# RWKV attention, a bilinear layer and a SoLU layer in one kernel: the second layer's transposes go to the DMA crossbar

## Chip, cores and metric

The kernel runs on one core of one Trainium2 chip. The metric is the device time of one launch in microseconds (us). The kernel before takes 664.51 us, the median of 3 runs (663.81 to 665.28).

## The reference, cut to what matters

```python
def _attn_ref(r, k, v, w, u):              # B, H, S, D = 4, 8, 768, 48
    for t in range(S):
        ...
        y[:, :, t] = np.einsum('bhd,bhde->bhe', rt, state + cur)
        state = w[None, :, :, None] * state + np.einsum('bhd,bhe->bhde', kt, vt)

def _moe_ref(x, w1, w2, w3, w_out):        # x: 3072 x 384, d_ff = 1024
    return ((x @ w1) * (x @ w2) @ w3) @ w_out

def _moe2_ref(x, w_in, w_out, g_ln):       # the "second layer", w_in 384 x 1024, w_out 1024 x 384
    h = x @ w_in
    e = np.exp(h - np.max(h, axis=-1, keepdims=True))
    sm = e / (np.sum(e, axis=-1, keepdims=True) + 1e-09)
    solu = h * sm
    mu = np.mean(solu, axis=-1, keepdims=True)
    var = np.mean((solu - mu) ** 2, axis=-1, keepdims=True)
    return ((solu - mu) / np.sqrt(var + 1e-06) * g_ln) @ w_out
```

Everything is float32. The change lies in `_moe2_ref` alone: between `solu - mu` (the "centred products") and the product with `w_out`.

## The kernel before, in words

The 3072 tokens are 24 chunks of 128 (NCH = 24). The first part of the kernel (attention and the bilinear layer) follows an order that a planner writes out; it ends near 440 us and is not touched. Its result, x for the second layer, lies in SBUF with features on the partitions. Every product is made of 32-bit floats split into a high and a low part (`split`, L525: ScalarE copies the high part into the fp32r type, VectorE subtracts it from the source for the low part), and `mm3` (L195) adds three matmuls per term: high by high, high by low, low by high (L199, L200, L201).

The second layer is the loop of L1170 over i, under a manual schedule: each engine runs its instructions in the order in which the code issues them, and waits only on semaphores. The steps are:

- `split_chunk(i + 2)`: x of the chunk two ahead is split, high part by ScalarE (`x2h`, L841), low part by GpSimd (`x2l`, L842).
- `s3(i + 1)`: 18 matmuls of 512 columns (2 halves, 3 k-tiles, 3 products) write `ps_h`, 128 tokens x 1024. VectorE takes the negated maximum (`nm`, L856), ScalarE the exponential `e` and its sum (L859), VectorE the product `p` (L863), its mean and variance (L866 to L876), GpSimd the factor `al` (L878, L880).
- `s4(i - 1)`: 24 matmuls of 384 columns (8 k-tiles, 3 products) of the transposed chunk with w_out, into `ps_o`; ScalarE scales the result by `al` into `o` (L920), and SyncE's queue (SP) stores it (L921).
- `turn(i)`, which is `s4_T(i)`: TensorE transposes the centred chunk with the identity, 8 blocks of 128x128 into two banks `ps_p` (L900); ScalarE and VectorE split each half out of PSUM into `pt` (L902).
- `center(i + 1)`: ScalarE writes p minus the mean over `e` (L885).

On TensorE the order of an iteration is thus s3(i + 1), s4(i - 1), T(i). The first iteration has T(0) between the halves of s3(1), the last one issues T(22) right behind the exponential of chunk 23, ahead of that chunk's statistics (`at == 2`, L860). After the loop come three quarters of s4(22), T(23), the last quarter, and s4(23).

Pools alternate by chunk parity (`pick(i)`): two `ps_h`, two `e`, two `p`; `pt` alternates between two places.

Of the kernel before, what the change touches and what calls it, by code (L numbers as in the profile page):

```python
# [8 lines left out]
F32 = mybir.dt.float32  # L9
F32R = mybir.dt.float32r  # L10
I32 = mybir.dt.int32
U32 = mybir.dt.uint32
AF = mybir.ActivationFunctionType
ALU = mybir.AluOpType
AX = mybir.AxisListType
# [108 lines left out]
def tile_rwkv_bilinear_solu(  # L124
# [19 lines left out]
    nc = tc.nc  # L144
    B, S, H, D = r.shape
    P = 128
    DP = 64
    NC = S // P
    NCH = B * NC
# [4 lines left out]
    KF = FF // P  # L154
    GT = B * P
    NH = FF // 2

    const = ctx.enter_context(tc.tile_pool(name="const", bufs=1, side="left"))
# [33 lines left out]
    def f32(ap):  # L192
        return ap.bitcast(F32)

    def mm3(dst, terms, start=True, stop=True):  # L195

        last = len(terms) - 1
        for i, ((ah, al), (bh, bl)) in enumerate(terms):
            nc.tensor.matmul(dst, lhsT=ah, rhs=bh, start=start and i == 0, stop=False)  # L199
            nc.tensor.matmul(dst, lhsT=ah, rhs=bl, start=False, stop=False)  # L200
            nc.tensor.matmul(dst, lhsT=al, rhs=bh, start=False, stop=stop and i == last)  # L201
# [37 lines left out]
    def same(n):  # L239

        return max([m for m in range(n) if slot(m) == slot(n)], default=-1)
# [94 lines left out]
    def diag(n, e=nc.vector):  # L336

        asb = asb_of(n)
        if e is nc.scalar:
            for h in range(H):  # L340
                nc.scalar.activation(asb[:, h, :], ident, AF.Copy, scale=bon[n][:, h:h + 1])
        else:
# [5 lines left out]
    def copy(e, dst, src):  # L348
        (e.copy if e is nc.scalar else e.tensor_copy)(dst, src)  # L349
# [134 lines left out]
    def cv_m(i):  # L484
        n = units[i][1][0] * units[i][1][1]
        hi = work[i]["s"][:, 0:n, 1].bitcast(F32)
        if i < NPS:
            m = psx.tile([P, UW], F32, name="cvp", tag=f"ps_x2{i % 3}")
            nc.scalar.activation(m[:, 0:n], hi, AF.Copy, scale=2.0 ** -112)
        else:  # L490
            m = cv.tile([P, UW], F32, name="cvm", tag="cvm", bufs=cmb)
            nc.scalar.activation(m[:, 0:n], hi, AF.Abs, scale=2.0 ** -112)
        work[i].update(m=m, mi=m[:, 0:n].bitcast(I32))

    def cv_q(i):
        n = units[i][1][0] * units[i][1][1]
        q = cv.tile([P, UW], I32, name="cvq", tag="cvq", bufs=cqb)
        nc.scalar.activation(q[:, 0:n], work[i]["s"][:, 0:n, 0].bitcast(U32), AF.Copy, scale=2.0 ** -29)
        work[i]["q"] = q[:, 0:n]
# [25 lines left out]
    def split(src, h, l):  # L525
        return (lambda e=nc.scalar: copy(e, h, src)), (lambda e=nc.vector: e.tensor_sub(l, src, f32(h)))  # L526

    def run(fns):
        for fn in fns:
            fn()  # L530
# [243 lines left out]
    def open_phase2():  # L774
# [14 lines left out]
        def split_wo(f, i):  # L789
            h, l = d2["woh"][:, i:i + 1, :], d2["wol"][:, i:i + 1, :]  # L790
            return (
                lambda: nc.scalar.activation(h, f, AF.Copy, scale=gc[:, i:i + 1]),
                lambda: nc.vector.scalar_tensor_tensor(
# [27 lines left out]
    pq = []  # L821
# [13 lines left out]
    def pick(i):  # L835
        return pq[i % len(pq)]
# [8 lines left out]
    def s3(x, i=0, between=None, at=1):  # L845
        xh, xl = x
        wih, wil = d2["wih"], d2["wil"]
        q = pick(i)["q"]
        ph = pick(i)["h"].tile([P, 2, NH], F32, name="ps_h", tag="ps_h")
        for hf in range(2):  # L850
            if between and hf == at:
                between()
            hsl = slice(hf * NH, (hf + 1) * NH)
            mm3(ph[:, hf, :], [((xh[:, kt, :], xl[:, kt, :]), (wih[:, kt, hsl], wil[:, kt, hsl])) for kt in range(KM)])
        nm = q.tile([P, 1], F32, name="nm", tag="nm")
        nc.vector.tensor_reduce(out=nm, in_=ph, axis=AX.XY, op=ALU.max, negate=True)  # L856
        e = q.tile([P, 2, NH], F32, name="e", tag="e")
        sm = q.tile([P, 1], F32, name="sm", tag="sm")
        nc.scalar.activation(e, ph, AF.Exp, bias=nm, scale=1.0, accum_out=sm)  # L859
        if between and at == 2:  # L860
            between()
        p = q.tile([P, 2, NH], F32, name="p", tag="p")
        nc.vector.tensor_mul(p, ph, e)  # L863
        st = q.tile([P, 2, 6], F32, name="bst", tag="bst")
        for hf in range(2):
            nc.vector.bn_stats(st[:, hf, :], p[:, hf, :])  # L866
        mv = q.tile([P, 2], F32, name="mv", tag="mv")
        nc.vector.bn_aggr(mv, st)
        nmean = q.tile([P, 1], F32, name="nmean", tag="nmean")
        nc.vector.tensor_scalar_mul(nmean, mv[:, 0:1], -1.0)  # L870
        c1 = q.tile([P, 1], F32, name="c1", tag="c1")
        nc.vector.tensor_scalar_add(c1, sm, 1e-9)
        nc.vector.reciprocal(c1, c1)
        vs = q.tile([P, 1], F32, name="vs", tag="vs")
        nc.vector.tensor_scalar(vs, mv[:, 1:2], c1, c1, op0=ALU.mult, op1=ALU.mult)
        nc.vector.tensor_scalar_add(vs, vs, 1e-6)  # L876
        rs = q.tile([P, 1], F32, name="rs", tag="rs")
        nc.gpsimd.tensor_tensor(rs, vs, pq[0]["nhalf"], op=ALU.pow)  # L878
        a = q.tile([P, 1], F32, name="al", tag="al")
        nc.gpsimd.tensor_mul(a, rs, c1)  # L880
        return e, p, nmean, a, i

    def center(st):
        e, p, nmean, a, i = st
        nc.scalar.activation(e, p, AF.Identity, bias=nmean, scale=1.0)  # L885
        return e, a, i

    def s4_T(pc):
        e, a, i = pc
        pv = e.rearrange("t a f -> t (a f)")  # L890
        if i % len(pq):
            t = const.tile([P, 2, KF, P], F32R, name="pt", tag="ox")
        else:
            t = pq[0]["q"].tile([P, 2, KF, P], F32R, name="pt", tag="pt")
        th, tl = t[:, 0], t[:, 1]
        for hf in range(2):
            ps = pick(hf)["p"].tile([P, KF // 2, P], F32, name="ps_p", tag="ps_p")
            for j in range(KF // 2):
                kf = hf * (KF // 2) + j
                nc.tensor.transpose(ps[:, j, :], pv[:, kf * P:(kf + 1) * P], ident)  # L900
            sl = slice(hf * (KF // 2), (hf + 1) * (KF // 2))
            run(split(ps, th[:, sl, :], tl[:, sl, :]))  # L902
        return th, tl, a, i

    def s4_mm(pT, ps, part, parts):
        th, tl = pT[:2]
        woh, wol = d2["woh"], d2["wol"]
        if part == 0:
            ps = pq[-1]["p"].tile([P, DM], F32, name="ps_o", tag="ps_o", bufs=len(pq))
        kfs = range(part * KF // parts, (part + 1) * KF // parts)  # L910
        mm3(
            ps, [((th[:, kf, :], tl[:, kf, :]), (woh[:, kf, :], wol[:, kf, :])) for kf in kfs],
            start=part == 0, stop=part == parts - 1,
        )
        return ps

    def s4_out(pT, ps, dst):
        a, i = pT[2:]
        o = pick(i)["q"].tile([P, DM], F32, name="o", tag="o")
        nc.scalar.activation(o, ps, AF.Copy, scale=a)  # L920
        nc.sync.dma_start(dst, o)  # L921

    def s4(pT, dst):
        s4_out(pT, s4_mm(pT, None, 0, 1), dst)

    def split_chunk(i):
        if i < NCH:
            xs[i] = x2_split(x2s(i).rearrange("t o m e -> t (o m) e"))

    def out_rows(i):  # L930
        c, b = divmod(i, B)
        row = b * S + c * P
        return out[row:row + P, :]

    xs, sm, pT = {}, {}, {}
    qsb, qps = ExitStack(), ExitStack()


# [28 lines left out]
    for n in range(NA + 2):  # L967
# [5 lines left out]
        p = same(n)  # L973
# [141 lines left out]
    for c in range(NG, NC):  # L1115
        last = c == NC - 1
        for ft in range(KF):
# [33 lines left out]
            if last and ft == KF - 1:  # L1151
                st = s3(xs[0])
# [14 lines left out]
    def turn(i):  # L1167
        pT[i] = s4_T(sm[i])

    for i in range(NCH - 1):  # L1170
        split_chunk(i + 2)
        within = i in (0, NCH - 2)
        st = s3(xs[i + 1], i + 1, (lambda: turn(i)) if within else None, 2 if i else 1)
        if i > 0:
            s4(pT[i - 1], out_rows(i - 1))
        if not within:
            turn(i)
        sm[i + 1] = center(st)
    ok = nc.values_load(wok[0:1, 0:1], min_val=0, max_val=1)
    i = NCH - 1  # L1180
    ps = None
    for j in range(4):
        if j == 3:
            turn(i)
        ps = s4_mm(pT[i - 1], ps, j, 4)
    s4_out(pT[i - 1], ps, out_rows(i - 1))
    s4(pT[i], out_rows(i))
    qps.close()
    qsb.close()
    sched.close()  # L1190
# [2 lines left out]
    with tc.If(ok < 1):  # L1193
# [8 lines left out]
        st = rp.tile([P, DE, D], F32, name="state")  # L1202
# [11 lines left out]
        with tc.For_i(0, S, TB) as t0:  # L1214
# [4 lines left out]
            for g in range(E4):  # L1219
                for b in range(B):  # L1220
                    sl = slice(g * BH + b * H, g * BH + (b + 1) * H)
# [24 lines left out]
        with tc.For_i(0, B * S, P) as row:  # L1246
# [6 lines left out]
            ps = pq[0]["p"].tile([P, KM, P], F32, name="ps_p", tag="ps_p")  # L1253
# [6 lines left out]
            for ft in range(KF):  # L1260
# [4 lines left out]
                a = gp.tile([P, P], F32, name="a")  # L1265
# [9 lines left out]
            xf = gp.tile([P, KM, P], F32, name="xf")  # L1275
            nc.scalar.copy(xf, px)
            s4(s4_T(center(s3(x2_split(xf)))), out[bass.ds(row, P), :])
        fx.close()
        rec.close()
# [63 lines left out]
```

## Time and profile before

| | |
|---|---|
| median of 3 runs | 664.51 us (663.81 to 665.28) |
| the profiled execution: span from first to last instruction | 662.6 us |
| TensorE busy | 648.3 us, 98% |
| VectorE, ScalarE, GpSimd busy | 411.6, 296.0, 260.1 us |
| DMA, whole kernel | 64.45 MB, mean 97 GB/s |
| second layer's loop | from about 440 us to 657.7 us |

The page gives no other time of the profiled execution than its span; it lies 1.9 us under the median of the unprofiled runs. A matmul's own duration covers its whole way through the array and overlaps its neighbours', so what a matmul costs is read from the distance of two starts, or from the chain of waits, not from its duration.

### The profile page before, as it was taken

Reading aid. Unit: us, or ns where it says so; the run is one execution under the profiler, and the core shown is the slowest. Engines: PE = TensorE matmul, PEld = TensorE weight load, DVE = VectorE, ACT = ScalarE, POOL = GpSimd, SP = SyncE. Lnnn points to the kernel's source line nnn. Section 1 sums busy time; section 2 is a strip of 40 time slices with the busy share of each in tenths; the row PEclk is TensorE's granted clock in tenths of the full one; section 3 lists DMA queues with packets and bytes.
Section 4 is the critical chain, followed back from the end, with each engine's and each line's share of the span. In section 5 each row is a group of like instructions: output and inputs, shape, how many; then the busy total and the mean of one; then the engine's idle time right before and its main releaser. Section 6 shows DMA issues by size and latency. Waiting matters only on the chain.

```text
span 662.6 us, 12211 instructions
## 1 busy us (share of the span) xinstructions
PE 648.3 (98%) x4820; PEld 555.6 (84%) x4820; DVE 411.6 (62%) x731; ACT 296.0 (45%) x600; POOL 260.1 (39%) x267
## 2 busy tenths in 40 slices
PE   8989999999999999999999999999999999999996
PEld 8767779998878888888888887879999999999996
DVE  8999999656753444344433477247666766667653
ACT  5575877553223222322232575344444534445442
POOL 3887655420345444555572555412222112221110
PEclk9999999999999999999999999999999999999999
DMA  8889696525452222222224132000000000000001
GB/s 285 256 281 294 222 301 200 189 90 152 144 155 69 68 68 69 69 68 69 72 81 124 69 119 72 0 1 12 25 25 26 24 13 25 24 25 25 13 24 41
DMA packets 44322, 64.45 MB, mean 97 GB/s; under 512 B 4833, under 2 KB 31202, under 8 KB 44258
## 3 DMA queue, kind: packets, MB, share of 16 engines
q1 hardware_dynamic: 44258, 63.60, 29.7%
q8 instruction: 40, 0.66, 0.4%
q14 instruction: 24, 0.20, 0.1%
HBM read 54.67 MB, written 8.91 MB: 96 GB/s over the span
## 4 chain that ended last, share of the span: by engine, by line
PE 84%; DVE 8%; ACT 2%; DMA 2%; issue 2%; POOL 2%; SPq 0%; DVEq 0%; POOLq 0%; ACTq 0%
PE ps_h L201 5%; PE ps_h L199 5%; PE ps_h L200 5%; PE ps_o L200 5%; PE ps_o L199 5%; PE ps_o L201 5%; PE ps_x L199 5%; PE ps_x L201 4%; PE ps_x L200 4%; PE ps_aa L199 4%; PE ps_bb L199 4%; PE ps_aa L200 4%; PE ps_aa L201 4%; PE ps_bb L200 4%; PE ps_bb L201 4%; PE ps_p L900 3%
## 5 line engine op out<-in xcount | busy, mean ns | idle before, releaser
L726 DVE TENSOR_TENSOR g<-ps_bb,a 128x512 f32<-128x512 f32 x48 | 33.0, 686 | 92.9 <-PE ps_bb L201 92.0
L511 POOL TENSOR_TENSOR cvm<-cvm,cvq 128x384 int32<-128x384 int32 (+1 forms) x54 | 66.8, 1244 | 41.9 <-DVE cvm L507 33.6
L878 POOL TENSOR_TENSOR rs<-vs,nhalf 128x1 f32<-128x1 f32 x24 | 13.0, 543 | 171.6 <-DVE vs L876 171.6
L737 POOL TENSOR_TENSOR gl<-g,gh 128x512 fp32r<-128x512 f32 x32 | 41.2, 1287 | 62.3 <-ACT gh L732 62.3
L199 PE MATMUL ps_o<-woh,pt 128*128 128x384 f32 x192 | 64.3, 335 | 0.0
L200 PE MATMUL ps_o<-wol,pt 128*128 128x384 f32 x192 | 64.3, 335 | 0.0
L201 PE MATMUL ps_o<-woh,pt 128*128 128x384 f32 x192 | 64.2, 334 | 0.0
L349 ACT COPY a<-ps_aa 128x512 f32<-128x512 f32 x46 | 26.9, 585 | 80.6 <-PE ps_aa L201 80.5
L199 PE MATMUL ps_bb<-x,w2h 128*128 128x512 f32 x144 | 57.2, 397 | 3.0 <-DVE g L726 3.0
L859 ACT ACTIVATE e<-ps_h,nm 128x1024 f32<-128x1024 f32 x24 | 26.8, 1117 | 73.2 <-DVE nm L856 73.2
L199 PE MATMUL ps_h<-wih,x2h 128*128 128x512 f32 x144 | 58.5, 406 | 0.0
L199 PE MATMUL ps_x<-gh,wc 128*128 128x512 f32 x144 | 58.3, 405 | 0.0
L199 PE MATMUL ps_aa<-x,w1h 128*128 128x512 f32 x144 | 57.2, 397 | 0.1
L201 PE MATMUL ps_h<-wih,x2l 128*128 128x512 f32 x144 | 56.6, 393 | 0.0
L200 PE MATMUL ps_aa<-x,w1h 128*128 128x512 f32 x144 | 56.2, 390 | 0.3 <-DVE x L526 0.3
L201 PE MATMUL ps_x<-gh,wc 128*128 128x512 f32 x144 | 56.3, 391 | 0.0
L200 PE MATMUL ps_h<-wil,x2h 128*128 128x512 f32 x144 | 56.2, 390 | 0.0
L201 PE MATMUL ps_bb<-x,w2l 128*128 128x512 f32 x144 | 56.1, 390 | 0.0
L201 PE MATMUL ps_aa<-x,w1l 128*128 128x512 f32 x144 | 56.1, 390 | 0.0
L200 PE MATMUL ps_x<-gl,wc 128*128 128x512 f32 x144 | 56.1, 390 | 0.0
L200 PE MATMUL ps_bb<-x,w2h 128*128 128x512 f32 x144 | 56.1, 390 | 0.0
L856 DVE TENSOR_REDUCE nm<-ps_h 128x1 f32<-128x1024 f32 x24 | 29.4, 1224 | 38.8 <-PE ps_h L201 38.8
(169 smaller groups left out, 1569.1 us busy)
## 6 DMA issues: line engine op xcount, KB each, us to landing
cvs<-in_w_T_dram SPq DMA_DIRECT2D x16, 512.0 KB, 4.3
cvs<-in_w_dram SPq DMA_DIRECT2D x16, 384.0 KB, 5.2
kT<-in_k_T_dram SPq DMA_DIRECT2D x20, 256.0 KB, 2.7
rT<-in_r_T_dram SPq DMA_DIRECT2D x20, 256.0 KB, 3.7
v_in<-in_v_dram SPq DMA_DIRECT2D x24, 192.0 KB, 3.9
k_in<-in_k_dram SPq DMA_DIRECT2D x24, 192.0 KB, 3.6
out_dram<-o SPq DMA_DIRECT2D x24, 192.0 KB, 1.9
gd<-g SPq DMA_DIRECT2D x16, 256.0 KB, 2.7
```

What stands on the lines that cost most here:

```text
L199: nc.tensor.matmul(dst, lhsT=ah, rhs=bh, start=start and i == 0, stop=False)
L200: nc.tensor.matmul(dst, lhsT=ah, rhs=bl, start=False, stop=False)
L201: nc.tensor.matmul(dst, lhsT=al, rhs=bh, start=False, stop=stop and i == last)
L349: (e.copy if e is nc.scalar else e.tensor_copy)(dst, src)
L511: nc.gpsimd.tensor_tensor(mi, mi, q, op=ALU.add)
L726: nc.vector.tensor_mul(gt[c, ft], pb, at[c, ft])
L737: e.tensor_sub(gl, g, f32(gh))
L856: nc.vector.tensor_reduce(out=nm, in_=ph, axis=AX.XY, op=ALU.max, negate=True)
L859: nc.scalar.activation(e, ph, AF.Exp, bias=nm, scale=1.0, accum_out=sm)
L878: nc.gpsimd.tensor_tensor(rs, vs, pq[0]["nhalf"], op=ALU.pow)
L900: nc.tensor.transpose(ps[:, j, :], pv[:, kf * P:(kf + 1) * P], ident)
```

## The change

From chunk 2 to chunk 22 (`M0 <= i < M1`, 21 chunks) `s4_T` is no longer called. In its place `move`, right behind `center`, does the following: ScalarE copies the 16-bit halves of `e` apart into the space of `p` (4 copies of 128x512, read with a step of two halves), SP stores each half of the chunk to HBM (256 KB each), and SP issues a transposing DMA for each, which reads rows of 512 16-bit numbers and writes them with features on the partitions back over `e`. `moved`, issued one iteration later, splits that tile from SBUF into `pt`. The product s4 of a chunk comes one iteration later than before. `e` now has three buffers. Chunks 0, 1 and 23 keep `s4_T`.

```diff
@@ s3
-        e = q.tile([P, 2, NH], F32, name="e", tag="e")
+        e = pq[min(i % 3, 1)]["q"].tile([P, 2, NH], F32, name="e", tag=f"e{i % 3}")
...
-        a = q.tile([P, 1], F32, name="al", tag="al")
+        a = q.tile([P, 1], F32, name="al", tag="al", bufs=2)
@@ center
-        return e, a, i
+        return e, a, i, p
+
+    def move(pc):
+
+        e, a, i, p = pc
+        ev = e.bitcast(U16).rearrange("t a (f k) -> t a f k", k=2)
+        pv = p.bitcast(U16).rearrange("t a (k f) -> t a k f", k=2)
+        d = pld.tile([2, P, 2, NH], U16, name="pd", tag="pd", bufs=2)
+        for hf in range(2):
+            for k in range(2):
+                nc.scalar.copy(pv[:, hf, k, :], ev[:, hf, :, k])
+            nc.sync.dma_start(d[hf], pv[:, hf])
+        x = e.rearrange("p a (k t) -> p (a k) t", t=P)
+        xv = x.bitcast(U16)
+        for hf in range(2):
+            sl = slice(hf * (KF // 2), (hf + 1) * (KF // 2))
+            nc.sync.dma_start_transpose(xv[:, sl, :], d[hf].rearrange("t k f -> (t k) f"))
+        return x, a, i
+
+    def pt_tile(i):
+        if i % len(pq):
+            return const.tile([P, 2, KF, P], F32R, name="pt", tag="ox")
+        return pq[0]["q"].tile([P, 2, KF, P], F32R, name="pt", tag="pt")
+
+    def moved(mv):
+        x, a, i = mv
+        t = pt_tile(i)
+        for hf in range(2):
+            sl = slice(hf * (KF // 2), (hf + 1) * (KF // 2))
+            run(split(x[:, sl, :], t[:, 0, sl, :], t[:, 1, sl, :]))
+        return t[:, 0], t[:, 1], a, i
@@ the loop
+    M0, M1 = 2, NCH - 1
     for i in range(NCH - 1):
         split_chunk(i + 2)
-        within = i in (0, NCH - 2)
-        st = s3(xs[i + 1], i + 1, (lambda: turn(i)) if within else None, 2 if i else 1)
-        if i > 0:
-            s4(pT[i - 1], out_rows(i - 1))
-        if not within:
+        st = s3(xs[i + 1], i + 1, None if i else (lambda: turn(0)))
+        if M0 <= i - 1:
+            pT[i - 1] = moved(pT[i - 1])
+        n = i - 1 if i <= M0 else i - 2
+        if n >= 0 and i != M0 + 1:
+            s4(pT[n], out_rows(n))
+        if 0 < i < M0:
             turn(i)
         sm[i + 1] = center(st)
+        if M0 <= i + 1 < M1:
+            pT[i + 1] = move(sm[i + 1])
     ok = nc.values_load(wok[0:1, 0:1], min_val=0, max_val=1)
-    i = NCH - 1
-    ps = None
-    for j in range(4):
-        if j == 3:
-            turn(i)
-        ps = s4_mm(pT[i - 1], ps, j, 4)
-    s4_out(pT[i - 1], ps, out_rows(i - 1))
-    s4(pT[i], out_rows(i))
+    pT[NCH - 2] = moved(pT[NCH - 2])
+    s4(pT[NCH - 3], out_rows(NCH - 3))
+    turn(NCH - 1)
+    for i in (NCH - 2, NCH - 1):
+        s4(pT[i], out_rows(i))
```

## Rows read from the trace of the kernel before

**Rows 1.** The page: busy time of each engine, share of the span, instructions.

```profile
PE 648.3 (98%) x4820; PEld 555.6 (84%) x4820; DVE 411.6 (62%) x731; ACT 296.0 (45%) x600; POOL 260.1 (39%) x267
```

**Rows 2.** Busy time per engine in one stretch of the loop, granted clock, DMA share, GB/s.

```profile
core 0: us, PE busy (x) PEld busy (x) DVE busy (x) ACT busy (x) POOL busy (x), PEclk, DMA share, GB/s
500.00:520.00 20.00, 20.00 (x111) 18.16 (x110) 13.36 (x32) 10.04 (x18) 3.52 (x6) 1.00 0.09 31
```

**Rows 3.** Chain of waits, 495 to 520 us: start, length in us, engine and line.

```profile
499.49 0.87 PE ps_p L900 x8
...
504.27 0.23 PE ps_h L201
...
508.67 0.87 PE ps_p L900 x8
```

**Rows 4.** Timeline of one chunk: start, us, engine, line, operation, idle before.

```profile
504.55 1.22 DVE L856 TENSOR_REDUCE nm<-ps_h 128x1 f32<-128x1024 f32 x1 [1.76 <-PE ps_h L201]
505.80 1.12 ACT L859 ACTIVATE e<-ps_h,nm 128x1024 f32<-128x1024 f32 x1 [3.23 <-DVE nm L856]
508.76 0.58 ACT L920 ACTIVATE o<-ps_o,al 128x384 f32<-128x384 f32 x1 [1.75 <-issue]
509.24 1.06 ACT L349 CAST pt<-ps_p 128x512 fp32r<-128x512 f32 x2
510.18 1.17 ACT L885 ACTIVATE e<-p,nmean 128x1024 f32<-128x1024 f32 x1
510.70 1.28 DVE L526 TENSOR_TENSOR pt<-ps_p,pt 128x512 fp32r<-128x512 f32 x2
511.24 0.52 ACT L841 CAST x2h<-x2b 128x384 fp32r<-128x384 f32 x1
511.83 1.03 POOL L842 TENSOR_TENSOR x2l<-x2b,x2h 128x384 fp32r<-128x384 f32 x1 [0.16 <-ACT x2h L841]
```

**Rows 5.** ScalarE and VectorE by operation and shape: total busy, mean ns, idle before.

```profile
L732 ACT CAST gh<-g 128x512 fp32r<-128x512 f32 x32 | 19.9, 621 | 59.7 <-DVE g L726 57.4 <-DVE nhalf L831 2.2
L498 ACT ACTIVATE cvq<-cvs 128x512 int32<-128x512 uint32 x22 | 14.9, 675 | 9.9 <-POOL cvm L511 8.0 <-DMA cvs<-in_w_T_dram 1.8
...
L526 DVE TENSOR_TENSOR wil<-cvm,wih 128x512 fp32r<-128x512 f32 x6 | 6.7, 1119 | 5.3 <-ACT wih L349 5.3
```

**Rows 6.** Timeline of ScalarE, two strided reads back to back.

```profile
381.14 0.67 ACT L492 ACTIVATE cvm<-cvs 128x512 f32<-128x512 f32 x1
381.70 0.67 ACT L498 ACTIVATE cvq<-cvs 128x512 int32<-128x512 uint32 x1
```

**Rows 7.** DMA issues of the page: count, KB each, median us to landing.

```profile
out_dram<-o SPq DMA_DIRECT2D x24, 192.0 KB, 1.9
gd<-g SPq DMA_DIRECT2D x16, 256.0 KB, 2.7
```

**Rows 8.** Instructions on tile gr (256 KB loads from HBM): us to landing.

```profile
DMA to landing us min/median/max: 2.5/2.9/6.2
```

**Rows 9.** Start of the loop: chain of waits (PE) and timeline of ScalarE.

```profile
462.77 0.87 PE ps_p L900 x8
...
457.11 1.15 ACT L885 ACTIVATE e<-p,nmean 128x1024 f32<-128x1024 f32 x1 [1.67 <-DVE c L872]
458.17 0.50 ACT L841 CAST x2h<-x2b 128x384 fp32r<-128x384 f32 x1
460.13 1.12 ACT L859 ACTIVATE e<-ps_h,nm 128x1024 f32<-128x1024 f32 x1 [1.47 <-DVE nm L856]
```

**Rows 10.** Timeline of the end, 642 to 658 us.

```profile
642.04 1.04 PE L900 MATMUL ps_p<-ident,e 128*128 128x128 f32 x8
642.24 1.23 DVE L856 TENSOR_REDUCE nm<-ps_h 128x1 f32<-128x1024 f32 x1 [1.75 <-PE ps_h L201]
...
650.05 0.34 PE L201 MATMUL ps_o<-woh,pt 128*128 128x384 f32 x1
...
650.69 1.09 PE L900 MATMUL ps_p<-ident,e 128*128 128x128 f32 x8 [0.31 <-ACT e L885]
```

More of the change, by code (lines that the diff above doesn't have):

```diff
@@ L12 @@
 U32 = mybir.dt.uint32
+U16 = mybir.dt.uint16
 AF = mybir.ActivationFunctionType
@@ L885, in center @@
         nc.scalar.activation(e, p, AF.Identity, bias=nmean, scale=1.0)
-        return e, a, i
+        return e, a, i, p
[25 more added lines that the diff above has]
+        return t[:, 0], t[:, 1], a, i
     def s4_T(pc):
-        e, a, i = pc
+        e, a, i, _ = pc
         pv = e.rearrange("t a f -> t (a f)")
[L891 to L894, printed above, removed]
+        t = pt_tile(i)
         th, tl = t[:, 0], t[:, 1]
@@ L935, in tile_rwkv_bilinear_solu @@
     xs, sm, pT = {}, {}, {}
+    pld = ctx.enter_context(tc.tile_pool(name="pld", bufs=1, space=bass.MemoryType.DRAM))
     qsb, qps = ExitStack(), ExitStack()
```

## Prediction

> **What bounds the kernel now.** I read the page's busy times first: TensorE is busy 98% of the span, every other engine under two thirds [rows 1]. An average says nothing about the stage that changes, so next comes the table of busy time by stretches: in the second layer's loop TensorE is busy 20.00 of 20 us at a granted clock of 1.00, VectorE 13.4, ScalarE 10.0, GpSimd 3.5, and the DMA engines 9% [rows 2]. There the clock is not in question, and whatever leaves TensorE shortens the loop until another engine's order of work ends later.
>
> The chain of waits gives what a chunk costs on TensorE. From one group of transposes to the next is 508.67 - 499.49 = 9.18 us: 0.87 for the eight transposes, 4.14 for s3 (500.36 to 504.50) and 4.17 for s4 (504.50 to 508.67) [rows 3].
>
> The timeline of one chunk gives the other engines' chain [rows 4]. VectorE takes the maximum at 504.55, ScalarE starts the exponential at 505.80 and centring at 510.18, and the next thing on ScalarE, the high part of x (x2h), starts at 511.24. From exponential to centring is 4.38 us, which is VectorE's product and statistics; in that gap ScalarE also does o and the two pt casts. The next exponential comes 9.18 us after the first, so ScalarE has slack.
>
> **The change part by part.** Terms are summed against the profiled execution, whose span of 662.6 us lies 1.9 us under the median of 664.51; I apply the difference to the median.
>
> *Transposes gone.* Chunks 2 to 22, 21 of 24, lose eight transposes: 21 x 0.87 = 18.3 us, all of it on the path. The period becomes 4.14 + 4.17 = 8.31 us if TensorE still bounds.
>
> *ScalarE's four copies, 84 in all.* They stand between centring and x2h. No row shows a 16-bit copy. Two rows bound the distance of their starts: two pt casts of 512 take 1.06 us together at about 0.59 each, a distance of 0.48 [rows 4]; centring, with 1024 numbers, holds ScalarE 1.06 (510.18 to 511.24), which is what a copy costs if skipping every other half costs a full read [rows 4]. The nearest row is a strided read of 512 numbers, which lasts 675 ns [rows 5], with starts 0.56 apart [rows 6]. I take 0.56. ScalarE and VectorE then have a closed round, from one exponential to the next: 4.38 to centring, 1.06 for it, 4 x 0.56 = 2.24, and 0.52 for x2h: 8.20 us. That is 0.11 under the 8.31 of TensorE, so I cost the copies at nothing in the steady loop, with hardly any cover: from 0.59 per copy on, ScalarE sets the period. At 0.48 the round is 7.9, at 1.06 it is 10.2.
>
> *Casts and subtractions of pt* stay 42 and 42 and read SBUF in place of PSUM. A cast from SBUF takes 0.62 [rows 5] against 0.59, inside the 4.38 us gap. VectorE's round from the maximum to the end of the subtractions is 511.98 - 504.55 = 7.43 [rows 4]. The dearest subtraction of this shape with both sources in SBUF took 1.12 [rows 5], against 0.64; two of those make 8.39, a tie with the period. I take nothing.
>
> *DMAs.* Per chunk two stores of 256 KB and two transposing DMAs of 256 KB, all on SP's queue, where only the output's store was. A store of that size (g to gd) lands in 2.7 us [rows 7], a load in 2.9 in the middle, 2.5 to 6.2 in all [rows 8]. No row shows a transposing DMA; the lower bound is 2.5, the upper the 6.2 of the slowest load, and I take 2.9, the median load, since it moves the same bytes. Room: the copies of a chunk end 4.38 + 1.06 + 2.24 = 7.7 us after its exponential starts; the split that needs the data stands on ScalarE behind the exponential two chunks on, at 2 x 8.31 + 1.2 = 17.8. That leaves 10.1 us, and 2.7 + 2 x 2.9 = 8.5 even in series. On the queue the transposes wait for the stores, and behind them waits the output's store of the chunk one further; its buffer is wanted again two chunks later, so nobody waits for it. Cost nothing; if they take over 4.2 us each one after the other, they set the period.
>
> The Trainium skill, "DMA: Bandwidth & Descriptors", section "Latency and other measured facts", gives a DMA transpose 261 GB/s; by that one of 256 KB is an estimated 1.0 us plus its fixed time, and the sum stays as it is. No row here shows one.
>
> *One chunk later, the start.* Iteration 3 has no s4, so s3(4) and s3(5) stand next to each other on TensorE, and x of chunk 5 must be split one s4 earlier. Before, centring of chunk 2 started at 457.11, x2h at 458.17, the exponential of chunk 3 at 460.13 [rows 9]. Now four copies and x2h of chunk 4 follow centring: 458.17 + 2.24 + 0.52 = 460.9, and exponential 3 starts there. Its centring starts 4.38 later, 465.3; with 1.06 + 2.24 + 0.52 x2h(5) ends at 469.1, and x2l takes GpSimd 1.03 more, 0.07 behind it [rows 4]: 470.2. TensorE has s4(1) done at 462.77 [rows 9], s3(4) at 466.9, two matmuls of s3(5) at 467.4, and the third needs x2l: it waits 2.8 us, once.
>
> *The end.* Chunk 23 keeps its transposes. s3(23) ends near 642.04 and its maximum starts 0.20 later [rows 10]. On VectorE the subtractions for chunk 21 now stand behind the statistics of chunk 23: they start 6.15 after the maximum (504.55 to 510.70 [rows 4]), the first half is there at 0.20 + 6.15 + 0.64 = 7.0 us after s3(23). TensorE has s4(20) in between and two matmuls of s4(21), 4.17 + 0.34 = 4.5, and waits 2.5. The wait of 0.47 ahead of T(23) (650.05 + 0.17 to 650.69 [rows 10]) goes, since 10 us lie between now: net 2.0.
>
> Sum: 18.3 - 2.8 - 2.0 = 13.5 us; 662.6 becomes 649.1, the median 651.0.
>
> **The rivals.**
>
> *A. ScalarE becomes the bound.* Its round is 5.96 + 4 times the copy. For it: the cover is 0.11 us, and copies that lasted their full 0.675 [rows 5] would make 8.66: 20 periods x 0.35 = 7 us, 658 us. At 0.75 per copy all gain is gone (664); at 1.06, 20 x 1.9 = 38 us, 689. Against it: starts on ScalarE are nearer than durations in every pair read [rows 4, 6].
>
> *B. The transposing DMAs set the pace, and the kernel gets slower.* They run one after the other on SP's queue, so a chunk takes twice one of them. From 4.2 us each they bind; from 4.5 (a period of 8.98, 20 x 0.67 = 13.5 us) the kernel is slower than before; at the slowest load, 6.2 [rows 8], the period is 12.4 and the time 651 + 20 x 4.1 = 733 us. For it: a transpose must write two-byte pieces across partitions. Against it: the DMA engines are 9% busy [rows 2], and plain transfers of the size take 2.7 to 2.9 [rows 7, 8].
>
> The Trainium skill speaks for B: "VectorE: DVE Perf Modes", section "The three transpose paths", gives the crossbar 1309 ns for one 128x128 block of 16-bit numbers, against 390 on TensorE. Eight blocks per DMA in a row would be an estimated 10.5 us, a period of 21 and some 900 us. No row of this case shows such a time.
>
> *C. The data come back later than 10.1 us, while the queue keeps up.* ScalarE then waits in front of the split, and two periods must hold the trip and what lies around it: 2.9 us beyond the room cost half of that per chunk, 20 x 1.45 = 29 us, 680. This needs a single transpose of some 5 us, so it goes with B.
>
> **How the numbers follow.** The forecast has a chance of 0.52, with its own range of 646 (no wait at start and end) to 656. A has 0.22: 0.16 of it still faster, 0.04 no change, 0.02 slower. B with C has 0.26, of which 0.02 ends faster, 0.01 within the bound and 0.23 slower. About 0.2% (1.3 us) is what a measurement of this kernel can tell from no change. Faster 0.70, same 0.05, slower 0.25. The range goes from 645 to 676, which takes in A up to a period of 9.6 and B up to 4.8 us per transpose, and leaves out about 0.2, nearly all of it above.
>
> **What would show it.** Right: starts of s3 8.3 us apart in the loop, TensorE busy in all of it; one wait of about 3 us near 467 us for x2l, one of 2.5 us in s4(21) for VectorE's subtraction; ScalarE's copies 0.56 apart, the exponential following x2h at once. The copies' duration decides A: look whether TensorE waits for x2l in every chunk. B shows as ScalarE or TensorE waiting for the DMA that writes e, in every chunk, and as transposes landing over 4 us after issue. The prediction is wrong if the period is above 8.5, or if the waits at both ends are not there.

## The result and the profile after

The changed kernel takes 656.21 us, the median of 4 runs (654.46 to 656.95), against 664.77 before: a ratio of 0.9862, with a 95% interval of 0.9842 to 0.9881. It is faster by 8.6 us by the medians (9.2 by the ratio), inside the range, and by about two thirds of the 13.5 us that were forecast. The profiled execution has a span of 652.8 us. Part of the difference to 662.6 lies ahead of the second layer, which the change does not touch: the first maximum of the loop starts at 434.29 where it started at 435.35.

The chain of waits of the kernel before, then of the kernel after: start, us, engine and line.

```profile
435.35 1.24 DVE nm L856
```

```profile
434.29 1.23 DVE nm L857
```

From there to the end of the span it was 227.25 us and is 218.51: the loop gained 8.7 us.

The page of the kernel after, busy time of each engine, which answers to [rows 1]; and its busy time by stretches, which answers to [rows 2].

```profile
PE 636.2 (97%) x4652; PEld 542.3 (83%) x4652; DVE 410.9 (63%) x731; ACT 344.7 (53%) x684; POOL 268.4 (41%) x267
```

```profile
core 0: us, PE busy (x) PEld busy (x) DVE busy (x) ACT busy (x) POOL busy (x), PEclk, DMA share, GB/s
...
460.00:480.00 20.00, 17.87 (x79) 14.89 (x79) 13.65 (x28) 13.87 (x24) 4.83 (x7) 0.91 0.69 148
...
500.00:520.00 20.00, 20.00 (x104) 18.36 (x103) 13.86 (x27) 15.77 (x27) 5.31 (x7) 1.00 0.60 155
...
620.00:640.00 20.00, 17.60 (x89) 16.42 (x88) 12.28 (x27) 10.80 (x18) 2.26 (x4) 0.91 0.49 107
```

In the steady loop TensorE is still busy all the time; ScalarE went from 10 to 16 of 20 us and the DMA engines from 9% to 60%. Between 460 and 640 us, TensorE is not full in two stretches, the two ends that the prediction named, and there the granted clock is 0.91.

TensorE's timeline in the steady loop, which answers to [rows 3]: the starts of s3, s4 and the next s3.

```profile
503.43 0.40 PE L200 MATMUL ps_h<-wih,x2h 128*128 128x512 f32 x1
...
507.63 0.34 PE L200 MATMUL ps_o<-woh,pt 128*128 128x384 f32 x1
...
511.82 0.40 PE L200 MATMUL ps_h<-wih,x2h 128*128 128x512 f32 x1
```

The period, from one s3 to the next, is 8.39 us, not 8.31: s3 takes 4.20 and s4 4.19, where they took 4.14 and 4.17. Fourteen periods, from the s4 at 482.47 to the one at 599.89, give 8.387.

ScalarE's timeline of one chunk, which answers to [rows 4].

```profile
508.29 0.51 ACT L842 CAST x2h<-x2b 128x384 fp32r<-128x384 f32 x1
509.09 1.11 ACT L860 ACTIVATE e<-ps_h,nm 128x1024 f32<-128x1024 f32 x1 [0.30 <-DVE nm L857]
...
510.20 1.13 ACT L350 CAST pt<-e 128x512 fp32r<-128x512 f32 x2
512.02 0.58 ACT L948 ACTIVATE o<-ps_o,al 128x384 f32<-128x384 f32 x1 [0.69 <-PE ps_o L202]
513.40 1.15 ACT L886 ACTIVATE e<-p,nmean 128x1024 f32<-128x1024 f32 x1 [0.80 <-DVE c L873]
514.59 2.18 ACT L897 COPY p<-e 128x512 uint16<-128x512 uint16 x4
516.67 0.51 ACT L842 CAST x2h<-x2b 128x384 fp32r<-128x384 f32 x1
517.48 1.12 ACT L860 ACTIVATE e<-ps_h,nm 128x1024 f32<-128x1024 f32 x1 [0.30 <-DVE nm L857]
```

The four copies take 2.18 us, each 0.62 long and with starts 0.52 apart, near the 0.56 that was taken. The exponential still waits 0.30 us for VectorE's maximum, which waits for TensorE: the round of the two engines is 8.39 - 0.30, about 8.1 us, and does not bind.

The DMA issues after: count, KB each, median us to landing.

```profile
pd<-p SPq DMA_DIRECT2D x42, 256.0 KB, 2.0
...
e<-pd SPq DMA_TRANSPOSE x42, 3.5
```

A transpose lands 3.5 us after its issue (3.1 to 4.7), between the 2.9 that was taken and the 4.2 at which transposes in series would have bound. The two of a chunk overlap, though: those issued at 509.70 and 510.98 landed at 513.04 and 514.39, and the split that reads them starts on ScalarE at 518.58.

The start of the loop, TensorE: s3(4) ends, s3(5) waits twice, and runs slowly for some matmuls.

```profile
465.69 0.40 PE L202 MATMUL ps_h<-wih,x2l 128*128 128x512 f32 x1
467.88 0.50 PE L200 MATMUL ps_h<-wih,x2h 128*128 128x512 f32 x1 [1.79 <-ACT x2h L842]
468.21 0.42 PE L201 MATMUL ps_h<-wil,x2h 128*128 128x512 f32 x1
468.97 0.80 PE L202 MATMUL ps_h<-wih,x2l 128*128 128x512 f32 x1 [0.34 <-POOL x2l L843]
469.56 0.63 PE L200 MATMUL ps_h<-wih,x2h 128*128 128x512 f32 x1
469.99 0.63 PE L201 MATMUL ps_h<-wil,x2h 128*128 128x512 f32 x1
...
472.00 0.39 PE L200 MATMUL ps_h<-wih,x2h 128*128 128x512 f32 x1
...
474.10 0.34 PE L200 MATMUL ps_o<-woh,pt 128*128 128x384 f32 x1
```

The end, TensorE: s4(20) and two matmuls of s4(21), the wait, slow matmuls, full speed again.

```profile
629.41 0.34 PE L201 MATMUL ps_o<-wol,pt 128*128 128x384 f32 x1
632.15 0.59 PE L202 MATMUL ps_o<-woh,pt 128*128 128x384 f32 x1 [2.40 <-DVE pt L527]
632.53 0.52 PE L200 MATMUL ps_o<-woh,pt 128*128 128x384 f32 x1
632.86 0.52 PE L201 MATMUL ps_o<-wol,pt 128*128 128x384 f32 x1
...
635.72 0.34 PE L201 MATMUL ps_o<-wol,pt 128*128 128x384 f32 x1
```

After either wait the matmuls start 0.43 us apart (512 columns) and 0.32 (384 columns) in place of 0.233 and 0.173. The granted clock from 469 to 471 us is 0.50: the lower of the two levels, 1.2 of 2.4 GHz, for 3.4 us at either end.

### The profile page after: what moved, and what is told of

Read it like the earlier page. It is cut to its first block, busy times and chain, and to the rows that moved or that the text cites. A ratio compares the mean times of both kernels' runs of the same rounds, so it can differ in the third digit from the quotient of the medians.

```text
span 652.8 us, 12151 instructions
## 1 busy us (share of the span) xinstructions
PE 636.2 (97%) x4652; PEld 542.3 (83%) x4652; DVE 410.9 (63%) x731; ACT 344.7 (53%) x684; POOL 268.4 (41%) x267
## 4 chain that ended last, share of the span: by engine, by line
PE 72%; DVE 12%; ACT 5%; POOL 4%; DMA 3%; issue 3%; SPq 0%; DVEq 0%; POOLq 0%; ACTq 0%
PE ps_o L202 5%; PE ps_o L200 5%; PE ps_o L201 5%; PE ps_h L202 5%; PE ps_h L201 4%; PE ps_h L200 4%; PE ps_x L200 4%; PE ps_x L202 4%; PE ps_x L201 4%; PE ps_aa L200 3%; PE ps_aa L202 3%; PE ps_aa L201 3%; PE ps_bb L200 3%; PE ps_bb L202 3%; PE ps_bb L201 3%; PE ps_a L369 3%
## 5 line engine op out<-in xcount | busy, mean ns | idle before, releaser
L202 PE MATMUL ps_o<-woh,pt 128*128 128x384 f32 x192 | 65.1, 339 | 2.4 <-DVE pt L527 2.4
L879 POOL TENSOR_TENSOR rs<-vs,nhalf 128x1 f32<-128x1 f32 x24 | 20.9, 872 | 111.0 <-DVE vs L877 111.0
L200 PE MATMUL ps_o<-woh,pt 128*128 128x384 f32 x192 | 65.2, 340 | 0.0
L733 ACT CAST gh<-g 128x512 fp32r<-128x512 f32 x32 | 19.9, 621 | 60.3 <-DVE g L727 58.1
L864 DVE TENSOR_TENSOR p<-ps_h,e 128x1024 f32<-128x1024 f32 x24 | 29.4, 1225 | 31.7 <-ACT e L860 31.7
```

The source lines that it names most:

```text
L733: nc.scalar.copy(gt[c, ft][1], gt[c, ft][0])
```

## The experiments

The question was where 4.8 of the 13.5 us went. **Theory:** into both ends, since the waits cost more than their own length, and into s3's spacing through the placement of its operands. **Rivals:** the DMA traffic slows TensorE's reads; ScalarE or the trip through HBM holds the loop up. Each ratio is against the kernel before on the same chip; the changed kernel has 0.9862 (0.9842 to 0.9881), and differences in us against it are of medians where nothing else is said.

**1. Placement, 64 bytes.** The change gave al a second buffer, which moved x2h and x2l by 32 bytes.

```diff
-        a = q.tile([P, 1], F32, name="al", tag="al", bufs=2)
+        a = q.tile([P, 1], F32, name="al", tag="al", bufs=3)
```

> The changed kernel with one thing more: the one-column tile al gets three buffers, which moves x2h and x2l by 32 bytes, back to addresses that 64 divides (155712 in place of 155744; 155776 before the change). Theory (placement): the 18 matmuls of s3 start 0.2286 us apart again and not 0.233, the period of the loop goes from 8.385 to about 8.31, 23 chunks x 0.08 = 1.9 us less than the changed kernel, about 654.3. Rival (traffic of the transposing DMAs, or the lack of transposes, slows the reads of TensorE): spacing and time stay, 656.2.

656.73 us, ratio 0.9869 (0.9847 to 0.9892). The starts of s3's matmuls lie 0.232 us apart, the period is 8.37. No gain: divisibility by 64 is not it.

**2. The split of x ahead of the copies.**

```diff
     for i in range(NCH - 1):
-        split_chunk(i + 2)
...
         sm[i + 1] = center(st)
+        split_chunk(i + 3)
         if M0 <= i + 1 < M1:
```

> The changed kernel with the split of x of chunk i+3 issued right behind centring of chunk i+1, ahead of ScalarE's four copies, in place of behind them. Theory (the wait and the slow clock behind it cost 4.0 us at the start): TensorE's wait near 466 us shrinks from 2.1 to some 0.3 us, the granted clock of 460 to 480 us goes from 0.91 to 1.00, and the time falls by 3.5 to 4.0 us, to about 652.5. Rival (only the wait itself counts, the clock falls by some other cause): 2.0 us less, 654.2, and the clock still falls. Rival (the transposed data are late then, or the exponential is held up): no gain.

655.03 us, ratio 0.9854 (0.9831 to 0.9877): by the time alone it can't be told from the changed kernel. The clock of 460 to 480 us is 1.00, as the theory had it, and s3(5) waits no more, but s4(2) does, for VectorE, which has the subtraction of chunk 2 behind the statistics of chunk 4. The line of TensorE's timeline in this kernel:

```profile
474.30 0.45 PE L202 MATMUL ps_o<-woh,pt 128*128 128x384 f32 x1 [2.14 <-DVE pt L527]
```

s3(4) and s3(5) together take 8.72 us in place of 12.38, and s4(2) takes 6.60 in place of 4.17: in the trace 1.2 us remain of 3.7. Neither the theory nor a rival named this outcome: the wait moved by one product.

**3. The last split ahead of the last statistics.**

```diff
+        def split_late():
+            pT[i - 1] = moved(pT[i - 1])
+        last = i == NCH - 2
-        st = s3(xs[i + 1], i + 1, None if i else (lambda: turn(0)))
+        st = s3(xs[i + 1], i + 1, split_late if last else None if i else (lambda: turn(0)), 2 if last else 1)
```

> The changed kernel with the split of chunk 21 issued right behind the exponential of chunk 23 and ahead of that chunk's statistics on VectorE. Theory: TensorE no longer waits 2.5 us in s4(21), its clock stays up there, and the time falls by 3.5 to 4.1 us, to about 652.4. Rival (the statistics of chunk 23 come later by 1.3 us and hold up its transposes and the last product): 2 us or less.

651.48 us, ratio 0.9817 (0.9791 to 0.9843). The gain against the changed kernel is 0.0045 of 664.8, 3 us by the ratios (4.7 by the medians, whose runs spread over 4 us), near the theory's 3.5 to 4.1, and the trace shows why: s4(20) and s4(21) take 8.69 us together in place of 12.61, and the clock of that stretch is 1.00.

```profile
620.00:640.00 20.00, 19.82 (x111) 18.57 (x111) 13.01 (x27) 11.48 (x20) 1.86 (x4) 1.00 0.47 109
```

**4. The three together.**

> The three edits together (al in three buffers, x split ahead of the copies, chunk 21 split ahead of the last statistics). Theory: the gains add up, 1.9 + 3.8 + 3.8 = 9.5 us under the changed kernel, about 646.7, and TensorE has no wait over 0.5 us in the loop from chunk 3 on. Rival (ScalarE's round takes over once TensorE is faster): the period stays over 8.35 and the time is above 648.

649.85 us, ratio 0.9779 (0.9752 to 0.9806), the fastest version, clear of the changed kernel's interval. The period is 8.37, TensorE's one long wait is 2.1 us in s4(2), and of the forecast 9.5 us some 5.5 are there by the ratios: the placement gave nothing, and the start gave 1.2. The period and the time are those of the rival, but not by its cause: from 480 to 620 us TensorE is busy all the time, so ScalarE's round did not take over.

**5. The kernel before, with the change's line for al alone.**

```diff
-        a = q.tile([P, 1], F32, name="al", tag="al")
+        a = q.tile([P, 1], F32, name="al", tag="al", bufs=2)
```

> The kernel before with one thing changed: al gets two buffers, which moves x2h and x2l by 32 bytes to the addresses that they have in the changed kernel. TensorE still transposes, and there is no added DMA. Theory (placement): s3's matmuls start 0.233 us apart in place of 0.2286, 24 chunks x 0.08 = 1.9 us, about 666.7. Rival (traffic): spacing and time as before, 664.8.

666.71 us, ratio 1.0025 (1.0011 to 1.0039): slower, as the theory had it. In this kernel, with TensorE's own transposes and the DMA engines at 6%, s3's matmuls start 0.233 to 0.234 us apart in place of 0.229, and the period is 9.25 in place of 9.18. The starts of s3 and s4 in this kernel, then in the kernel before:

```profile
502.50 0.48 PE L199 MATMUL ps_h<-wih,x2h 128*128 128x512 f32 x1
...
506.77 0.34 PE L199 MATMUL ps_o<-woh,pt 128*128 128x384 f32 x1
```

```profile
628.64 0.48 PE L199 MATMUL ps_h<-wih,x2h 128*128 128x512 f32 x1
...
632.87 0.33 PE L199 MATMUL ps_o<-woh,pt 128*128 128x384 f32 x1
```

From s3 to s4 that is 4.27 us (4.27 to 4.29 in other chunks) against 4.23.

**6. No trip through HBM.** Leaves out the stores and the transposing DMAs.

```diff
-            nc.sync.dma_start(d[hf], pv[:, hf])
...
-            nc.sync.dma_start_transpose(xv[:, sl, :], d[hf].rearrange("t k f -> (t k) f"))
```

> The changed kernel without its 42 stores and 42 transposing DMAs: ScalarE still copies the halves, and the split reads the centred chunk as it is, so the data that go into the last product are not transposed. Theory (the trip through HBM is hidden): the period stays 8.385 us and the time 656.2, within 1 us. Rival (traffic or the queue costs something per chunk): the period falls to 8.31 or below and the time by 1.5 us or more.

656.15 us, ratio 0.9869 (0.9850 to 0.9887): the time of the changed kernel. Busy time from 480 to 620 us, first of the changed kernel, then of this one:

```profile
480.00:620.00 140.00, 140.00 (x704) 126.39 (x703) 99.18 (x199) 110.72 (x186) 36.45 (x51) 1.00 0.58 150
```

```profile
480.00:620.00 140.00, 140.00 (x701) 126.07 (x701) 100.74 (x204) 110.10 (x187) 35.26 (x51) 1.00 0.07 25
```

The DMA share falls from 58% to 7%, s3's spacing stays at 0.233 and the period at 8.39. The trip is hidden, and its traffic costs TensorE nothing that can be seen.

**7. Every transpose twice.**

```diff
+        yv = p.rearrange("p a (k t) -> p (a k) t", t=P).bitcast(U16)
+        for hf in range(2):
+            sl = slice(hf * (KF // 2), (hf + 1) * (KF // 2))
+            nc.sync.dma_start_transpose(yv[:, sl, :], d[hf].rearrange("t k f -> (t k) f"))
```

> The changed kernel with every transposing DMA issued a second time, into the space of p, where nobody reads it. In the changed kernel the DMA engines are 59% busy in the loop, against 6% before, which makes about 2.1 us of all 16 engines for one transpose. Theory (the engines are the limit of the DMAs, and they work on two transposes at a time): four take some 8.5 us and the two stores 1, so the DMAs set a period of 9.0 to 9.6, and the time goes up by 10 to 25 us, to 666 to 681. Rival (one after the other at their 3.5 us to landing): a period of 14 us, about 770. Rival (hidden with room to spare): 656.

668.96 us, ratio 1.0076 (1.0056 to 1.0096): 12.8 us over the changed kernel, inside the theory's range. The period is 9.03 on average (16 of them from 482.82 to 627.34), far from the 14 of transposes in series, the DMA engines are 82% busy, and VectorE's product waits for the second transposes into p. The line of the waits from 480 to 640 us gives us in total, times and the longest:

```profile
480.00:640.00 160.00, 152.28 (x748) 133.50 (x747) 104.82 (x216) 112.80 (x195) 37.64 (x53) 1.00 0.82 195
```

```profile
DVE p L864 <- DMA p<-pd: 21.0, 6, 4.5
```

So in rival B's terms there is room for one transpose per half, but not for two: 0.82 x 9.03 - 0.58 x 8.39 = 2.5 us of all DMA engines for two more transposes, 1.3 each. Whether the DMA engines themselves set this pace is not shown: the wait for p is one that only the doubled kernel has, since it alone writes there.

**8. Six copies in place of four.**

```diff
-                nc.scalar.copy(pv[:, hf, k, :], ev[:, hf, :, k])
+                for rep in range(2 if hf else 1):
+                    nc.scalar.copy(pv[:, hf, k, :], ev[:, hf, :, k])
```

> The changed kernel with two of the four 16-bit copies done twice, six per chunk in place of four. Theory: ScalarE and VectorE's round, which is 8.1 us by the trace of the changed kernel (0.30 us of idle time in a period of 8.39), grows by 2 x 0.53 to 9.15 and sets the period: 20 x 0.76 = 15 us more, about 671. Rival (ScalarE has more slack than the closed round says, as the exponential can slip): under 5 us more.

677.77 us, ratio 1.0201 (1.0183 to 1.0219): 21.6 us over the changed kernel. The period is 9.29, and ScalarE has no gap left from the copies to the exponential:

```profile
500.81 0.51 ACT L842 CAST x2h<-x2b 128x384 fp32r<-128x384 f32 x1
501.23 1.11 ACT L860 ACTIVATE e<-ps_h,nm 128x1024 f32<-128x1024 f32 x1
...
506.71 3.48 ACT L898 COPY p<-e 128x512 uint16<-128x512 uint16 x6
510.10 0.51 ACT L842 CAST x2h<-x2b 128x384 fp32r<-128x384 f32 x1
510.52 1.11 ACT L860 ACTIVATE e<-ps_h,nm 128x1024 f32<-128x1024 f32 x1
```

The six take 1.30 us more than the four, and 9.29 - 1.30 = 7.99 us is the round without them, near the 8.1 read above. Rival A was 0.3 to 0.4 us away. The rest over the forecast 15 us is the dearer pair of copies and both ends: s3(4) and s3(5) take 15.20 us in place of 12.38, s4(20) and s4(21) 14.95 in place of 12.61.

**9. The product not one chunk later.**

```diff
-        n = i - 1 if i <= M0 else i - 2
-        if n >= 0 and i != M0 + 1:
+        n = i - 1
+        if n >= 0:
```

> The changed kernel with its product not one chunk later: s4 of a chunk follows in the same iteration in which its split is issued, as in the kernel before. Theory (the delay is needed, since the split stands on VectorE behind the next chunk's statistics): s4 gets its low part 7.0 us after s3 ends in place of 0.5, so a period has 4.2 + 7.0 + 3.8 = 15 us, 20 x 6.6 = 132 us more, about 790, and TensorE's clock falls in every chunk, which adds some more. Rival (the trip through HBM and not the order on VectorE is what the delay covers): TensorE waits for the DMA, and the period is longer than 17.

821.43 us in a single run. TensorE waits twice in every chunk, for ScalarE's cast and for VectorE's subtraction, never for a DMA; the period is 17.0 us, and the granted clock of the loop lies between 0.76 and 0.83.

```profile
554.01 0.44 PE L200 MATMUL ps_o<-woh,pt 128*128 128x384 f32 x1 [3.06 <-ACT pt L350]
557.89 0.69 PE L202 MATMUL ps_o<-woh,pt 128*128 128x384 f32 x1 [3.26 <-DVE pt L527]
```

What TensorE waits for is the order on VectorE and ScalarE, not the trip. The forecast 15 us had both waits right (s3 and they take 11.3 us, from 546.58 to 557.89) and left out the slower matmuls, of which it gave no size: the last 22 of s4 take 5.75 us in place of 3.8.

**10. Placement, 128 bytes.** As 1, with five buffers.

> The changed kernel with al in five buffers, which moves x2h and x2l to addresses that 128 divides, as they had before the change (155648, 157184, 158720, 160256; before 155776, 157312, 158848, 160384). With three buffers (64 divides them, 128 does not) s3's matmuls stayed at 0.2325 us. Theory (placement of the weights relative to 128 bytes): 0.2286 again, a period of 8.31 and about 1.8 us less than the changed kernel, 654.4. Rival (the shift alone is not the cause; the loop without transposes also slows s3): 0.2325 to 0.233 and 656.2.

655.47 us, ratio 0.9858 (0.9827 to 0.9888), spacing 0.233, period 8.38: the rival's numbers. Divisibility by 128 is not it either.

**11. All edits, and chunk 2 split early as well.**

```diff
+        early = i in (M0 + 1, NCH - 2)
+        st = s3(xs[i + 1], i + 1, split_late if early else None if i else (lambda: turn(0)), 2 if early else 1)
```

> The changed kernel with four edits: al in five buffers, the split of x ahead of ScalarE's copies, and the splits of chunks 2 and 21 issued right behind the exponential, ahead of the statistics of chunks 4 and 23 on VectorE. In the runs so far the early split of x took the wait from s3(5), and 2.1 us of it came back in s4(2), which waited for VectorE's subtraction of chunk 2. Theory: that wait goes too, TensorE has no wait over 0.5 us from chunk 3 on, and against the changed kernel 1.8 (placement) + 4.0 (start) + 4.1 (end) = 9.9 us go, about 646.5. Rival (the data of chunk 2 are not back by then, or the wait moves once more): 648 to 650.

652.35 us, ratio 0.9809 (0.9781 to 0.9837), no better than experiment 4. s4(2) now takes 4.64, but s3(6) takes 4.93 and s4(3) 6.57: statistics and copies of chunk 4 came later, and the wait moved once more, as the rival had it, with a time above the rival's 648 to 650.

**12. The kernel before, moved by 128 bytes.** As 5, with five buffers.

> The kernel before with al in five buffers: x2h and x2l move by 128 bytes, so that 128 still divides their addresses. Theory (placement relative to 128 bytes): s3's matmuls start 0.2286 apart, 664.7 as before. Rival (any move, or the other tiles that move along, slows the kernel, as the move by 32 bytes did): 0.233 and 666.7.

666.92 us, ratio 1.0027 (1.0007 to 1.0046), spacing 0.233, period 9.26: the rival's numbers. The theory that 128 bytes decide falls here too.

## Why the prediction was right, and where its sum was not

- **Transposes gone, 18.3 us.** Right in place and mechanism. The period that was to be left, 8.31, assumed that a matmul of s3 costs what it did. It measured 8.387, 1.4 us in 18 periods. Experiments 5 and 12 show that the line for al alone, with no transposing DMA in the kernel, brings the slower spacing; it stands in the changed kernel from s3(0) on (0.233 from 429.9 us), before the first transposing DMA. What the edits share is that x2h, x2l and other tiles of the two pools that hold al lie at other addresses, by 32, 64 or 128 bytes; s4, whose operands (pt and w_out) stay where they were, does not differ by more than 0.03 us. Which property of the old addresses made s3 faster is open: divisibility by 64 and by 128 were tried and are not it.
- **The copies, nothing.** Right: 0.52 apart, and experiment 8 shows both that ScalarE binds soon after and at which round. One sign did not come: the exponential does not follow x2h at once but 0.30 us later, since TensorE and not ScalarE sets the period.
- **Casts and subtractions, nothing.** Right: with both sources in SBUF a subtraction took 0.69 us, far from the 1.12 of [rows 5], and the two start 0.60 apart (1.29 for both).
- **The DMAs, nothing.** Right (experiment 6), though the price was a guess from plain loads. The landing time of 3.5 us was above the 2.9 taken, and the premise that transposes run one after the other on SP's queue, on which rival B's bound of 4.2 us stands, did not hold: the two of a chunk are issued 1.28 us apart and both land within 4.7 us. The Trainium skill, "VectorE: DVE Perf Modes", section "The three transpose paths", gives 1309 ns for one block; eight in a row would be an estimated 10.5 us, but one DMA of eight blocks landed in 3.5 us here. The Trainium skill's 261 GB/s in "DMA: Bandwidth & Descriptors", section "Latency and other measured facts", is nearer: 256 KB in 1.3 us of all engines is an estimated 206 GB/s by experiment 7.
- **The start, 2.8 us.** It cost 4.0: 12.38 us for s3(4) and s3(5), against 2 x 4.20. The waits are 1.79 us for x2h and 0.34 for x2l with some latency, about 2.5; the rest is the lower clock behind them. That there are two is in the prediction's own times, by which x2h ends at 469.1, and the first two matmuls need it as well; the sum is the same. The clock was not in the sum. In experiments 6, 7 and 10 the same two waits (about 1.8 and 0.34 to 0.37) were followed by matmuls at full speed, and the pair took 11.08 us; in experiments 1 and 3 they were followed by slow ones, as in the changed kernel. Whether the clock falls after such a wait thus differs between profiles, and no run shows why. At full speed s4(2) in turn waits 0.3 us (4.50 in experiments 6 and 10), so the start costs 3.0 us there, close to the 2.8, and the lower clock added 1.0. Of the 1.2 us that experiment 2 gained, all but 0.3 (11.08 + 4.50 against 8.72 + 6.60) is therefore this clock, not the wait. The step also missed what lay behind it. TensorE leaves out one s4, 4.2 us of its work, while the other engines still need their 8 us per chunk. In each order of these steps that was run the lead was waited for, with 2.7 to 4.0 us in all: in s3(5), in s4(2) (experiment 2), or in s4(2), s3(6) and s4(3) (experiment 11).
- **The end, 2.0 us net.** The wait was 2.57 us, as forecast (2.5), but ten matmuls behind it ran at the lower clock: 635.72 - 632.15 = 3.57 us for 11 starts in place of 1.9, 1.7 us more. Experiments 3, 4 and 11 take the wait away, and the slow clock goes with it; in the profiles of experiments 1, 2, 6 and 10, which keep the wait, the clock falls behind it each time.

These three make 1.4 + 1.2 + 1.7 = 4.3 of the missing 4.8 us; another 0.2 is the slower spacing from s3(0) to s3(3). The path and the terms were right and their sizes were not: the two ends were priced as waits alone, and TensorE's own pace was taken as fixed when tiles moved.

## What to carry to other kernels

A wait on a full TensorE costs its length and, behind about half of the waits of 1.8 to 2.5 us in these profiles (always at the end, never in s4(2)), 3.4 us at the lower clock, which is up to 1.7 us more; price both. When work is skewed by one step, the engine that gets ahead may have to wait once wherever the first wait is moved, as it did in all orders tried here: read the round of the other engines before mending it. A move to DMA is free only as long as the engine that prepares the data has room, here 0.3 us per chunk of 8.4.

## What was not expected of the hardware

- A buffer of 4 bytes per partition more in a pool, and with it operands 32 bytes further down, made s3's matmuls 2% slower (0.229 to 0.233 us), and the kernel before 0.25% slower (experiment 5).
- A transposing DMA holds SP's queue for 1.29 us at issue, against 0.33 for a plain one; two of them take 2.57 on the queue's timeline.
- GpSimd's rs, on one column, takes 0.94 us in place of 0.54 where VectorE's subtraction of pt, now with both sources in SBUF, runs beside it (rs 505.75 to 506.69, subtractions 505.60 to 506.89). It is off the path, and the cause was not tried.
